# Half of batch 1's second product as seven block products, DVE's work of that stretch reordered, and the states' rows read two batches together

## The chip, the cores and the metric

The kernel runs on one core of a Trainium2 chip. The metric is the device time of one execution in microseconds, lower is better. TensorE (PE) multiplies into PSUM, VectorE (DVE) and ScalarE (ACT) compute and empty PSUM, GpSimd (POOL) copies and adds between SBUF tiles, and SyncE (SP) issues most of the DMAs. Each engine takes its instructions in the order in which the program issues them, and semaphores order the engines among each other.

## What is computed

For each of 8 batches and 8 heads, x (512 rows of 64) and state (32 rows of 64) read each other by attention; the 544 rows of each batch then go through a feed-forward layer, 512 to 2048 to 512, with a leaky ReLU.

```python
scores = scale * np.matmul(x, state.transpose(0, 1, 3, 2))
a = softmax(scores); xread = np.matmul(a, state)        # 512 rows a batch
scores2 = scale * np.matmul(state, x.transpose(0, 1, 3, 2))
a2 = softmax(scores2); sread = np.matmul(a2, x)         # 32 rows a batch
rows = np.concatenate([xread, sread], axis=2)           # heads side by side: 512 columns
h = rows @ w_in; out = np.maximum(0.01 * h, h) @ w_out
```

## The kernel before, in words

All five engines follow an order written out by hand (manual_schedule): the program's text is each engine's queue. bfloat16 goes into the products, PSUM holds float32.

Work on the 512 rows of a batch. a_scores writes both heads' score halves (the "sc" bank pair). For x's rows, a_shift takes the maximum per block of 32 (block_max), spreads it (a transpose) and subtracts it, a_exp is ACT's exp, and a_probs sums, inverts, spreads and multiplies into aT. For the states' rows, a_max2, a_exp2 (ACT, with the sum accumulated) and a_probs2 give a2, which a_a2t transposes by DMA on SP. xread is never formed: a_m multiplies the state by w_in into M (four chunks of 512 columns, each copied out of PSUM by ACT or DVE), and ff1 multiplies aT by M and applies the leaky ReLU on ACT, writing hT, 16 slots of 128 columns.

The second product, hT by w_out, has two forms. piece is the plain one: four matmuls of 512 columns for a block of 128 rows, four pieces to a block. Fast, with Batch on top, is Strassen's scheme in Winograd's form, seven block products for eight: weights_sum makes four sums of blocks of w_out (tw), Fast.sums makes four sums of blocks of hT (su) on DVE, unit is one step of one product (two matmuls of 256 columns for a batch's 512 rows), save copies a bank to SBUF on ACT, join adds a bank and a saved one on DVE, and one addition goes to POOL. Two banks ("py") carry the seven products, in the order 1, 2, 6, 5, 7, 3, 4: products 6 and 3 add into the bank in which products 1 and 5 already stand, after those were saved.

The main loop runs over b = 2 to 7, and over 16 slots s in each. Slot s holds ff1 of batch b for 128 columns, and a filling of second-product units: of batch b - 1, and from about slot 10 of batch b itself (PACE). The next batch's attention (nxt) lies on DVE and ACT in the same slots: a_scores and a_shift in slot 1, a_max2 in slot 3, a_exp in 5, a_exp2 and a_probs in 7 and 8, a_probs2 in 11; three chunks of its M come in slot 10. ff1, the rows' product and chunk 2 of M share the two "ph" banks in turn. Batches 0 and 1 come ahead of the loop. Batch 0's second product and batch 1's are done by pieces; of batch 1's, six pieces lie ahead of the loop and the last ten in slots 0 to 9 of b = 2 (the list std).

The states' 32 rows are read by a_sread_rows: 32 small matmuls per batch (a2T by xb), copied by ACT to sr_n and transposed by DMA (sread_t) into sr_t; batch 7's by a_sread. It is called for batch 0 in slot 1 of b = 2, for batches 1 and 2 in slot 10 of b = 2, and for batch b in slot 10 of b = 3 to 6. All states' rows go through the feed-forward layer together at the end (FastIn and fs).

## Time and profile before

| | |
|---|---|
| three runs | 204.59, 204.79, 205.09 us; median 204.79 |
| the profiled execution | 204.49 us, of which the span in the profile is 202.7 |
| busy in the span | PE 197.0 us, DVE 151.4, ACT 143.7, POOL 39.7 |
| granted TensorE clock | 1.0 |
| bytes moved by DMA | 27.99 MB |
| PE matmuls of 128x256 in the second products, one | 109 ns apart |
| PE matmuls of 128x512, one | 216 ns apart |

A row of the timeline gives start and duration in us, engine, line of the kernel, operation, output tile from input tiles, shape, and how many are merged into it; a bracket gives idle time ahead of it and the engine that ended it. A row of a group gives the total, the mean duration in ns and the idle time ahead. Durations of matmuls overlap one another, so starts are used for them.

### The profile page before, as it was taken

Reading aid. Unit: us, or ns where it says so; the run is one execution under the profiler, and the core shown is the slowest. Engines: PE = TensorE matmul, PEld = TensorE weight load, DVE = VectorE, ACT = ScalarE, POOL = GpSimd, SP = SyncE. Lnnn points to the kernel's source line nnn. Section 1 sums busy time; section 2 is a strip of 40 time slices with the busy share of each in tenths; the row PEclk is TensorE's granted clock in tenths of the full one; section 3 lists DMA queues with packets and bytes.
Section 4 is the critical chain, followed back from the end, with each engine's and each line's share of the span. In section 5 each row is a group of like instructions: output and inputs, shape, how many; then the busy total and the mean of one; then the engine's idle time right before and its main releaser. Section 6 shows DMA issues by size and latency. Waiting matters only on the chain.

```text
span 202.7 us, 4755 instructions
## 1 busy us (share of the span) xinstructions
PE 197.0 (97%) x1964; PEld 126.0 (62%) x1964; DVE 151.4 (75%) x230; ACT 143.7 (71%) x265; POOL 39.7 (20%) x66
## 2 busy tenths in 40 slices
PE   7899999999999999999999999999999999999993
PEld 2543544444344567766776767766767677799882
DVE  1677679599799969976996699769968853686612
ACT  3458848589869796978697878788778856467710
POOL 8831002021005005200251040200020002004250
PEclk9999999999999999999999999999999999999999
DMA  6999996999477895537946795250017100410035
GB/s 189 223 207 277 229 298 113 141 303 245 53 175 214 114 275 109 103 125 253 118 29 181 240 127 105 103 159 5 0 57 198 27 0 32 178 55 0 3 89 170
DMA packets 39733, 27.99 MB, mean 138 GB/s; under 512 B 25312, under 2 KB 36704, under 8 KB 39712
## 3 DMA queue, kind: packets, MB, share of 16 engines
q1 hardware_dynamic: 34512, 20.88, 44.6%
q0 software_dynamic: 4912, 6.55, 15.8%
q10 hardware_dynamic: 288, 0.26, 0.6%
q8 instruction: 15, 0.25, 0.5%
q14 instruction: 6, 0.05, 0.1%
HBM read 17.30 MB, written 8.91 MB: 129 GB/s over the span
## 4 chain that ended last, share of the span: by engine, by line
PE 96%; DVE 1%; ACT 1%; issue 0%
PE yq L557 36%; PE ph L372 23%; PE py L487 10%; PE pm L351 4%; PE pyw L487 3%; PE pf L441 3%; PE yu L557 3%; PE pspin L132 3%; PE ph L804 2%; PE sc L206 1%; PE psn L318 1%; PE phw L383 1%; PE php L804 1%; DVE M L365 1%; ACT xT L666 1%; PE scn L695 0%
## 5 line engine op out<-in xcount | busy, mean ns | idle before, releaser
L377 ACT ACTIVATE hT<-ph 128x512 bf16<-128x512 f32 x108 | 63.5, 604 | 22.0 <-PE ph L372 21.4
L372 PE MATMUL ph<-aT,M 128*128 128x512 bf16 x216 | 62.3, 379 | 0.0
L557 PEld LDWEIGHTS <-su 128*128 128x128 bf16 x416 | 39.7, 98 | 14.5 <-DVE su L546 1.7
L557 PEld LDWEIGHTS <-hT 128*128 128x128 bf16 x288 | 27.7, 98 | 11.7 <-issue 1.1
L557 PE MATMUL yq<-tw_xf,su 128*128 128x256 bf16 x192 | 27.2, 273 | 0.0
L105 POOL CAST xb<-xl 128x512 bf16<-128x512 f32 (+1 forms) x21 | 14.4, 724 | 65.2 <-PE ph L372 40.6
L557 PE MATMUL yq<-w_out_bf,hT 128*128 128x256 bf16 x192 | 27.0, 273 | 0.0
L372 PEld LDWEIGHTS <-M 128*128 128x128 bf16 x216 | 21.0, 98 | 9.3 <-issue 0.8
L546 DVE TENSOR_TENSOR su<-hT 128x1024 bf16<-128x1024 bf16 x24 | 16.8, 700 | 10.5 <-ACT hT L377 10.5
L487 PE MATMUL py<-w_out_bf,hT 128*128 128x512 bf16 x96 | 24.2, 379 | 0.0
L487 PEld LDWEIGHTS <-hT 128*128 128x128 bf16 x128 | 12.1, 98 | 14.6 <-issue 0.9
L627 POOL TENSOR_TENSOR yo<-sv,sv 128x512 f32<-128x512 f32 x6 | 7.8, 1300 | 54.1 <-ACT sv L566 42.7
L569 DVE TENSOR_TENSOR yo<-yq,sv 128x512 f32<-128x512 f32 x17 | 11.6, 685 | 6.5 <-PE yq L557 6.5
L566 ACT COPY sv<-yq 128x512 f32<-128x512 f32 x24 | 13.9, 585 | 2.0 <-PE yq L557 1.4
L365 ACT CAST M<-pm 128x1024 bf16<-128x1024 f32 x13 | 13.2, 1014 | 0.9 <-PE pm L351 0.8
L557 PE MATMUL yq<-w_out_bf,su 128*128 128x256 bf16 x96 | 13.1, 273 | 0.0
L557 PE MATMUL yq<-tw_x,su 128*128 128x256 bf16 x96 | 13.1, 272 | 0.0
L557 PE MATMUL yq<-tw_x,hT 128*128 128x256 bf16 x88 | 12.1, 273 | 0.0
L274 ACT ACTIVATE e<-sc,mcols 128x512 bf16<-128x512 f32 x16 | 11.1, 696 | 0.0
L216 DVE TRANSPOSE_TENSOR_REDUCE mrow<-sc 128x32 f32<-128x1024 f32 x7 | 8.7, 1245 | 2.4 <-PE sc L206 2.4
L266 DVE TENSOR_REDUCE mcol<-sc 128x2 f32<-128x1024 f32 x8 | 9.7, 1215 | 0.0
L247 DVE STREAM_TRANSPOSE qb<-qh 128x1024 bf16<-128x1024 bf16 x7 | 8.7, 1245 | 0.2
(147 smaller groups left out, 271.3 us busy)
## 6 DMA issues: line engine op xcount, KB each, us to landing
xl<-in_x_dram SPq DMA_DIRECT2D x5, 1024.0 KB, 7.1
out_dram<-yo SPq DMA_DIRECT2D x10, 512.0 KB, 3.0
w_in_bf<-in_moe_w_in_dram POOLq DMA_DIRECT2D x4, 512.0 KB, 9.1
w_out_bf<-in_moe_w_out_dram POOLq DMA_DIRECT2D x4, 512.0 KB, 17.0
out_dram<-ysb SPq DMA_DIRECT2D x8, 256.0 KB, 5.1
xf<-in_x_dram SPq DMA_DIRECT2D x2, 512.0 KB, 4.8
x<-in_x_dram POOLq DMA_DIRECT2D x2, 512.0 KB, 13.8
xl<-in_x_dram POOLq DMA_DIRECT2D x1, 1024.0 KB, 19.8
```

The costliest lines, as they stand in the source:

```text
L105: copy(xs[b][:, :, h0:h1].rearrange("p t h d -> p h t d"), xl[b][:, h0:h1].rearrange("p h (t d) -> p h t d", t=NT),)
L216: nc.vector.tensor_reduce(out=m1[:], in_=flat.rearrange("p (c j) -> p c j", j=NS), axis=AX.X, op=ALU.max, apply_transpose=True,)
L266: nc.vector.tensor_reduce(out=m2[:], in_=a.sc[:], axis=AX.X, op=ALU.max, negate=True)
L274: nc.scalar.activation(out=a.e2[:, g], in_=a.sc[:, g, :], func=AF.Exp, bias=a.m2s[:, g:g + 1], scale=SCALE, accum_out=a.r2[:, g:g + 1],)
L365: copy(a.M[:, :, cols], pm[:])
L372: nc.tensor.matmul(ph[:], lhsT=a.M[:, g, P * j:P * (j + 1)], rhs=a.aT[:, g, :], start=(g == 0), stop=(g == 1),)
L377: nc.scalar.activation(out=hT[:, j, :], in_=ph[:], func=AF.Prelu, alpha=0.01)
L487: nc.tensor.matmul(y.py, lhsT=hT[:, j, P * i:P * (i + 1)], rhs=w_out_bf[:, j, :], start=(j == 0), stop=(j == 15),)
L546: (eng or nc.vector).tensor_tensor(out=S[n][:, ms], in0=u[:, ms], in1=v[:, ms], op=op)
L557: nc.tensor.matmul(bank[:, i, :], lhsT=lhs[:, m, P * i:P * (i + 1)], rhs=rhs[:, m, :], start=(first and m == 0 and (i == 0 or of is not No ...
L566: copy(t[:], bank)
L569: nc.vector.tensor_tensor(out=dst, in0=bank, in1=self.sv[n][:], op=ALU.add)
```

## The change

Rows 256 to 511 of batch 1's h1 (a block of two row blocks) take a new class Half: the seven block products with one 128-row matmul per unit (56 matmuls of 256 columns) in place of eight pieces, seven units a slot in slots 2 to 9 of b = 2. Its sums, saves and joins come with it. The sums of w_out move ahead: two to the end of batch 0, one to the end of batch 1, one to slot 4 of b = 2. In b = 2 the next batch's attention is spread anew: the row maxima's spreading in slot 1, the subtraction and a_max2 in slot 4, a_exp in 6, a_exp2 in 8 and 9, a_probs' reciprocal in 9 and its multiplication after slot 10's copies. For batches 0 to 6, a2 stays unnormalised (a2 is e2 itself), its reciprocals are kept in qall, and DVE multiplies them in when it copies the rows' product out of PSUM, where ACT copied before. The rows of batches 1 and 2, 3 and 4, 5 and 6 are read together, in slot 1 of b = 3, 5 and 7. e2 and a2T have three buffers, sread_t takes three batches and then four, and the order of the two "py" banks is turned in even batches instead of odd ones.

```diff
@@ -140,6 +140,7 @@
     st_t = [consts.tile([P, hi - lo, P], BF16, name=f"st_t{lo}") for lo, hi in groups]
     sr_t = consts.tile([P, B, NK, NS], BF16, name="sr_t")
     sr_n = {}
+    qall = consts.tile([P, B, 2], FP32, name="qall")
     stb0 = consts.tile([P, 4, D], BF16, name="stb0")
@@ -219,9 +220,12 @@
         )
         return m1
-    def block_sub(flat, m1, n):
+    def block_rows(m1, n):
         m1b = att.tile([P, n, NS], FP32, name="mrowb", tag="mrowb", bufs=1)
         nc.vector.transpose(m1b[:], m1[:, :, None].to_broadcast([P, n, NS]))
+        return m1b
+
+    def block_sub(flat, m1b, n):
         sh = att.tile([P, n * NS], FP32, name="sh", tag="sh", bufs=1)
         nc.vector.tensor_tensor(
             out=sh[:], in0=flat, in1=m1b[:].rearrange("p c j -> p (c j)"), op=ALU.subtract,
@@ -233,7 +237,7 @@
         nc.scalar.activation(out=e1[:], in_=sh[:], func=AF.Exp, scale=SCALE)
         return e1
-    def block_probs(dst, e1, n):
+    def block_recip(e1, n):
         r1 = att.tile([P, n], FP32, name="r1", tag="r1")
         nc.vector.tensor_reduce(
             out=r1[:], in_=e1[:].rearrange("p (c j) -> p c j", j=NS),
@@ -243,6 +247,9 @@
         q1h = att.tile([P, n], BF16, name="qh", tag="qh")
         with nc.allow_low_precision(reason="one rounding, of the finished reciprocal"):
             nc.vector.reciprocal(q1h[:], r1[:])
+        return q1h
+
+    def block_probs(dst, e1, q1h, n):
         q1b = att.tile([P, n, NS], BF16, name="qb", tag="qb", bufs=1)
         nc.vector.transpose(q1b[:], q1h[:, :, None].to_broadcast([P, n, NS]))
         nc.vector.tensor_tensor(
@@ -250,16 +257,22 @@
             in1=q1b[:].rearrange("p (g c) j -> p g (c j)", g=2), op=ALU.mult,
         )
-    def a_shift(a):
+    def a_shift(a, part=None):
         flat = a.sc[:].rearrange("p g c -> p (g c)")
-        a.sh = block_sub(flat, block_max(flat, NB), NB)
+        if part != 1:
+            a.mb = block_rows(block_max(flat, NB), NB)
+        if part != 0:
+            a.sh = block_sub(flat, a.mb, NB)
     def a_exp(a):
         a.e1 = block_exp(a.sh, NB)
-    def a_probs(a):
-        a.aT = att.tile([P, 2, S], BF16, name="aT", tag="aT")
-        block_probs(a.aT[:], a.e1, NB)
+    def a_probs(a, part=None):
+        if part != 1:
+            a.q1h = block_recip(a.e1, NB)
+        if part != 0:
+            a.aT = att.tile([P, 2, S], BF16, name="aT", tag="aT")
+            block_probs(a.aT[:], a.e1, a.q1h, NB)
     def a_max2(a):
         m2 = att.tile([P, 2], FP32, name="mcol", tag="mcol")
@@ -269,7 +282,7 @@
     def a_exp2(a, g):
         if g == 0:
-            a.e2 = att.tile([P, 2, S], BF16, name="e2", tag="e2")
+            a.e2 = att.tile([P, 2, S], BF16, name="e2", tag="e2", bufs=3)
             a.r2 = att.tile([P, 2], FP32, name="r2", tag="r2")
         nc.scalar.activation(
             out=a.e2[:, g], in_=a.sc[:, g, :], func=AF.Exp,
@@ -278,17 +291,19 @@
     def a_probs2(a):
         nc.vector.tensor_scalar(out=a.r2[:], in0=a.r2[:], scalar1=1e-9, scalar2=None, op0=ALU.add)
-        q2 = att.tile([P, 2], FP32, name="qc", tag="qc")
-        nc.vector.reciprocal(q2[:], a.r2[:])
-        a.a2 = att.tile([P, 2, S], BF16, name="a2", tag="a2")
-        for g in range(2):
-            nc.vector.tensor_scalar(
-                out=a.a2[:, g, :], in0=a.e2[:, g, :],
-                scalar1=q2[:, g:g + 1], scalar2=None, op0=ALU.mult,
-            )
+        q2 = qall[:, a.b]
+        nc.vector.reciprocal(q2, a.r2[:])
+        a.a2 = a.e2
+        if a.b == B - 1:
+            a.a2 = att.tile([P, 2, S], BF16, name="a2", tag="e2", bufs=3)
+            for g in range(2):
+                nc.vector.tensor_scalar(
+                    out=a.a2[:, g, :], in0=a.e2[:, g, :],
+                    scalar1=q2[:, g:g + 1], scalar2=None, op0=ALU.mult,
+                )
     def a_a2t(a):
-        a.a2T = att.tile([P, 2, NT, P], BF16, name="a2T", tag="a2T")
+        a.a2T = att.tile([P, 2, NT, P], BF16, name="a2T", tag="a2T", bufs=3)
         nc.sync.dma_start_transpose(
             a.a2T[:].rearrange("p g i q -> p (g i) q"), a.a2[:].rearrange("p g s -> p (g s)")
         )
@@ -320,16 +335,18 @@
                             lhsT=a.a2T[:, g, i, NS * k:NS * (k + 1)], rhs=a.xb[:, i, 2 * k + g, :],
                             start=(i == 0), stop=(i == NT - 1),
                         )
-        c, b0 = divmod(some[0].b, 4)
+        c, b0 = (0, some[0].b) if some[0].b < 3 else (1, some[0].b - 3)
         if c not in sr_n:
             sr_n[c] = consts.tile([P, 4, P], BF16, name=f"sr_n{c}", tag=("st0f", "stf2")[c])
-        nc.scalar.copy(
-            sr_n[c][:, b0:b0 + len(some)], ps[:].rearrange("p u g d -> p u (g d)")
+        u0, n = some[0].b, len(some)
+        nc.vector.tensor_tensor(
+            out=sr_n[c][:, b0:b0 + n].rearrange("p u (g d) -> p u g d", g=2), in0=ps[:],
+            in1=qall[:, u0:u0 + n, :, None].to_broadcast([P, n, 2, D]), op=ALU.mult,
         )
     def sread_t(c, n):
         nc.sync.dma_start_transpose(
-            sr_t[:, 4 * c:4 * c + n].rearrange("p b k n -> p b (k n)"),
+            sr_t[:, 3 * c:3 * c + n].rearrange("p b k n -> p b (k n)"),
             sr_n[c][:, :n].rearrange("p b q -> p (b q)"),
         )
@@ -527,7 +544,7 @@
         def __init__(self, hT, q, homes, saved):
             self.q, self.sub = q, q // P
-            hv = hT[:].rearrange("p (m k) s -> p m k s", k=2)
+            hv = hT.rearrange("p (m k) s -> p m k s", k=2)
             self.A = {(r, k): hv[:, :, k - 1, q * (r - 1):q * r] for r in (1, 2) for k in (1, 2)}
             self.homes, self.saved, self.S = homes, saved, {}
             self.sv = {}
@@ -575,7 +592,7 @@
     class Batch:
         def __init__(self, b, hT):
             saved = {n: (spool, t, 1) for n, t in ((1, "sv1"), (6, "sv6"), (5, "sv1"), (7, "sv7"))}
-            self.b, self.f = b, Fast(hT, 2 * P, [(spool, f"su{n}", 1) for n in range(4)], saved)
+            self.b, self.f = b, Fast(hT[:], 2 * P, [(spool, f"su{n}", 1) for n in range(4)], saved)
             self.units = [(n, m) for n in (1, 2, 6, 5, 7, 3, 4) for m in range(NM)]
             own = [(n, m) for n in (1, 2) for m in range(6)] + [(1, 6), (2, 6), (1, 7)]
             assert len(own) == OWN
@@ -596,8 +613,8 @@
         def open(self, n):
             if n in (1, 2):
                 if not self.bank:
-                    ts = [psum.tile([P, 2, HC], FP32, name="yq", tag="py") for _ in range(2)]
-                    if self.b % 2:
+                    ts = [psum.tile([P, self.f.sub, HC], FP32, name="yq", tag="py") for _ in range(2)]
+                    if self.b % 2 == 0:
                         ts.reverse()
                     for k, t in zip((1, 2), ts):
                         self.bank[k] = t[:]
@@ -635,6 +652,22 @@
             elif n == 4:
                 f.join(self.yo(1)[:, :, :HC], bank, 7)
                 self.out(1)
+
+    class Half(Batch):
+
+
+        def __init__(self, hT):
+            super().__init__(1, hT)
+            self.f.__init__(hT[:, :, 2 * P:], P, self.f.homes, self.f.saved)
+            self.units = [(n, m) for n in (1, 2, 6, 5, 7, 3, 4) for m in range(NM)]
+
+        def yo(self, r):
+            if r not in self.yos:
+                self.yos[r] = ypool.tile([P, 1, DM], FP32, name="ysb", tag="ysb", bufs=3)
+            return self.yos[r]
+
+        def out(self, r, cols=slice(0, DM), i=None, eng=nc.sync):
+            eng.dma_start(rows_of(1)[2 + r], self.yo(r)[:, 0, :])
     OWN = 15
     PACE = (1, 4, 4, 4, 3, 4, 4, 3, 4, 4, 4, 4, 3, 4, 3, 3)
@@ -888,6 +921,9 @@
         cast_x(3, h, h + 2, POO)
     a_probs2(a0)
     a_a2t(a0)
+    weights_open()
+    weights_sum(2)
+    weights_sum(1)
@@ -919,6 +955,7 @@
     a_probs2(a2)
+    weights_sum(0)
     pm = [a_m(a2, 1, "big"), a_m(a2, 2, "sc")]
     m_evict(a2, 1, pm[0], VEC)
     m_evict(a2, 2, pm[1], SCA)
@@ -927,8 +964,7 @@
-    before = None
-    weights_open()
+    before, half = None, Half(h1)
     for b in range(2, B):
         hT = hpool.tile([P, 16, S], BF16, name="hT", tag="hT")
         a = att_of[b]
@@ -936,7 +972,9 @@
         now = Batch(b, hT)
         std = []
         if b == 2:
-            std = [(i, 3) for i in range(2)] + [(i, jq) for i in range(2, NT) for jq in range(4)]
+            std = [(i, 3) for i in range(2)]
+            for n in (0, 1):
+                half.f.sums(n)
         def fill(s):
             n = (PACE2 if b == 2 else PACE)[s]
@@ -953,7 +991,6 @@
             if s == 0:
                 if b + 2 < B:
                     load_x(b + 2, nc.sync)
-                    open_xb(b + 2)
                 a_a2t(a)
                 if before:
                     for n in (0, 1):
@@ -964,9 +1001,15 @@
                 m_evict(a, 3, a_m(a, 3, "big"), SCA)
                 if b == 2:
                     a_sread_rows([a0])
-                if nxt is not None:
+                elif b % 2:
+                    a_sread_rows([att_of[b - 2], att_of[b - 1]])
+                if b == 2:
+                    half.f.sums(2)
+                    a_shift(nxt, 0)
+                elif nxt is not None:
                     a_shift(nxt)
                 if b + 2 < B:
+                    open_xb(b + 2)
                     for h in range(0, H, 2):
                         cast_x(b + 2, h, h + 2, POO)
                 if before:
@@ -974,24 +1017,18 @@
             elif s == 3:
                 if before:
                     before.f.sums(3)
-                if nxt is not None:
+                if nxt is not None and b > 2:
                     a_max2(nxt)
-                if b == 2:
-                    weights_sum(0)
-                    weights_sum(2)
             elif s == 4:
                 if b == 2:
                     state_t(1)
                 elif b == 4:
-                    sread_t(0, 4)
+                    sread_t(0, 3)
                 elif b == 7:
-                    sread_t(1, 3)
+                    sread_t(1, 4)
             elif s == 8:
                 if nxt is None:
                     a_sread(a)
-                if b == 2:
-                    weights_sum(1)
-                    weights_sum(3)
             elif s == 12:
                 for n in range(3):
                     now.f.sums(n, 0, 4)
@@ -1007,7 +1044,12 @@
                 a_open(att_of[b + 2], b + 2)
                 a_xt_dma(att_of[b + 2])
             if nxt is not None:
-                if s == 5:
+                if b == 2 and s < 11:
+                    if s == 6:
+                        a_exp(nxt)
+                    elif s in (8, 9):
+                        a_exp2(nxt, s - 8)
+                elif s == 5:
                     a_exp(nxt)
                 elif s in (7, 8):
                     a_exp2(nxt, s - 7)
@@ -1020,16 +1062,26 @@
             if std:
                 i, jq = std.pop(0)
                 piece(1, h1, i, jq)
+            elif b == 2 and half.units:
+                half.run(7)
+                if s == 4:
+                    a_shift(nxt, 1)
+                    half.f.sums(3)
+                    weights_sum(3)
+                    a_max2(nxt)
+                elif s == 9:
+                    a_probs(nxt, 0)
             elif s != 11:
                 fill(s)
             if s == 10 and nxt is not None:
-                a_sread_rows([a1, a2] if b == 2 else [a])
                 pm0 = a_m(nxt, 0, "big")
                 pm1 = a_m(nxt, 1, "sc")
                 pm2 = a_m(nxt, 2, "ph")
                 for g, copy in enumerate((VEC, SCA)):
                     copy(nxt.M[:, g, 2 * DM:3 * DM], pm2[g][:])
                 m_evict(nxt, 0, pm0, SCA)
+                if b == 2:
+                    a_probs(nxt, 1)
         before = now
@@ -1038,8 +1090,8 @@
     hs = hpool.tile([P, 16, B * NS], BF16, name="hs", tag="hT")
     for n in (0, 1):
         before.f.sums(n, 4, 8)
-    fs = Fast(hs, P, [(att, "sh", 1), (att, "mrowb", 1), (att, "xT", 2), (att, "xT", 2)],
-              {1: (att, "e1", 1), 6: (att, "qb", 1), 5: (att, "e2", 2), 7: (att, "e2", 2)})
+    fs = Fast(hs[:], P, [(att, "sh", 1), (att, "mrowb", 1), (att, "xT", 2), (att, "xT", 2)],
+              {1: (att, "e1", 1), 6: (att, "qb", 1), 5: (att, "e2", 3), 7: (att, "e2", 3)})
     fi.hT = hs
     for n in (1, 2, 6, 5, 7, 3, 4):
         for r in range(2):
```

## Prediction

> **What bounds the kernel now.** I read the page's busy shares first, then the chain of waits in order of time, then the timeline of TensorE, DVE and ACT around the stretch that is changed.
>
> ```profile
> PE 197.0 (97%) x1964; PEld 126.0 (62%) x1964; DVE 151.4 (75%) x230; ACT 143.7 (71%) x265; POOL 39.7 (20%) x66
> PEclk9999999999999999999999999999999999999999
> PE 96%; DVE 1%; ACT 1%; issue 0%
> ```
>
> TensorE is busy for 97% of the span at the full granted clock, and the chain that ended last is 96% TensorE. From the start times of its matmuls I took each step minus that form's usual step: after 20 us it hardly waits for another engine, apart from the three short waits of term (c). So the end moves by the TensorE time removed, less any new wait on TensorE.
>
> ```profile
> 33.34 3.45 PE pyw L487 x16
> 67.01 0.63 PE psn L318 x64
> 189.64 6.11 PE yu L557 x56
> ```
>
> In these lines of the chain, 16 matmuls of 512 columns take 3.45 us (216 ns each), 64 of the rows' product 0.63, and 56 of 256 columns 6.11 (109 each). The last is exactly the form that the change puts in: seven products of eight matmuls, on the states' rows.
>
> ```profile
> 65.76 0.59 PE L372 MATMUL ph<-aT,M 128*128 128x512 bf16 x2
> 66.19 0.82 PE L557 MATMUL yq<-w_out_bf,hT 128*128 128x256 bf16 x6
> 66.94 0.70 PE L318 MATMUL psn<-xb,a2T 128*32 128x64 bf16 x64
> 67.57 0.99 PE L351 MATMUL pm<-w_in_bf,st_t 64*32 64x512 bf16 x24
> 68.49 0.83 PE L557 MATMUL yq<-w_out_bf,hT 128*128 128x256 bf16 x6
> 69.28 1.02 PE L372 MATMUL ph<-aT,M 128*128 128x512 bf16 x4
> 70.14 0.60 PE L557 MATMUL yq<-w_out_bf,hT 128*128 128x256 bf16 x4
> 70.70 0.59 PE L372 MATMUL ph<-aT,M 128*128 128x512 bf16 x2
> ```
>
> This is TensorE's timeline at slots 10 to 13 of stage 2 (the pass of the loop with b = 2); starts are what counts.
>
> **The removed and added TensorE work.**
>
> (a) Eight pieces of four matmuls (32 x 0.2156 = 6.90) become 56 of 256 columns (6.11): -0.79. A slot of slots 2 to 9 shrinks from 1.295 (55.40 to 65.76 over eight) to 0.432 + 7 x 0.109 = 1.195. From this, slot 2 still starts at 55.40, slot 6 at 60.18, slot 7 at 61.38, and slot 10 would at 64.96.
>
> The Trainium skill, TensorE: Matmul & The Clock Gate, Part 3 (The mechanism), says that a weight load overlaps running matmuls only where the row groups differ, which would speak against more and narrower matmuls. The trace disagrees: 56 full-height loads of 98 ns lie beside the 6.11 us.
>
> (b) Rows' products. Before: 64 in slot 10 of stage 2 (66.94 to 67.57, 0.63) and 32 in slot 10 of stages 3 to 6 (87.54 to 87.89, 0.35 each): 2.03. After: 64 in slot 1 of stages 3, 5 and 7. The 32 of batch 0, in slot 1 of stage 2 before and after, cost 0.34 (54.18 to 54.52); 32 more cost 0.63 - 0.35 = 0.28; so 0.62 each, 1.86. Net -0.17.
>
> (c) Three waits of stage 2 go with what made them. The pm group takes 0.92 (67.57 to 68.49) against 0.80 in stage 3 (87.89 to 88.69), for ACT's late psn copy. At 69.28 six matmuls of 0.109 should have been over at 69.15: DVE's copy of pm2[0], queued behind two weight sums, started only at 68.61. At 70.70 TensorE is 0.12 late behind an ACT queue that the psn copy had set back. Together -0.37.
>
> **What new waits cost.** The other engines take their work in the order issued, so I walked each queue with start-to-start times of the old trace.
>
> ```profile
> 59.92 0.60 ACT L377 ACTIVATE hT<-ph 128x512 bf16<-128x512 f32 x1 [0.70 <-PE ph L372]
> 60.41 1.05 ACT L233 ACTIVATE e<-sh 128x1024 bf16<-128x1024 f32 x1
> 61.36 0.58 ACT L497 COPY ysb<-py 128x512 f32<-128x512 f32 x1
> ```
>
> (d) In slot 6 ACT's queue is ff1's relu, a_exp (moved from slot 5), then save(5). The relu starts 0.64 after its first matmul (56.69 to 57.33 in the old trace): 60.82. The exp starts 0.49 later (59.92 to 60.41), 61.31; save(5) another 0.95 later (60.41 to 61.36), 62.26, and takes the 0.372 of the 128x256 copies of sv at L566: 62.63, with 0.06 for the release 62.69. The third product adds into the bank that save(5) reads, and TensorE is there at 61.38 + 0.432 + 5 x 0.109 = 62.36. **+0.33.** Nothing else of TensorE is between; before, eight pieces used no save.
>
> ```profile
> 45.96 1.23 DVE L238 TRANSPOSE_TENSOR_REDUCE r<-e 128x32 f32<-128x1024 bf16 x1
> 47.22 0.18 DVE L242 TENSOR_SCALAR r<-r 128x32 f32<-128x32 f32 x1
> 47.44 0.35 DVE L245 RECIPROCAL qh<-r 128x32 bf16<-128x32 f32 x1
> 68.61 0.69 DVE L1031 CAST M<-pm 128x512 bf16<-128x512 f32 x1 [0.26 <-PE pm L351]
> ```
>
> (e) In slot 9 a_probs' first part stands behind the join of the fourth product, which needs the last of the 56 matmuls, and DVE's copy of pm2[0] stands behind both; ff1 of slot 11 needs that bank. From the end of slot 9: 0.20 to the join (a copy starts 0.31 after the last matmul's start), 0.345 for it (0.424 at L569 on 128x256, the next starts 0.08 earlier), 1.27 + 0.22 + 0.27 for reduce, scalar and reciprocal, 0.67 of the copy (ff1 started at 69.28): 2.975. TensorE needs, without psn and (c), 69.28 - 65.76 - 0.63 - 0.25 = 2.62. **+0.35.**
>
> (f) Stage 1: DVE idles 1.61 us before its reduce at 40.66. Two weight sums there (L523, 1.14 and 1.25 apart) replace two multiplies (0.62) and run 0.1 over; ACT follows and ff1's banks have no slack at 49.85. Bounds 0 and 0.16; I take **+0.05**, as ACT had 0.04 in hand.
>
> **Edits costed at nothing.** The first weight sum (1.23) ends at 51.5, under the 0.99 us that DVE waited for pm at 51.71; uncovered it would hold only M columns that slot 4 needs. The multiplies of a2 (0.62 per batch) go from an engine that idles 1.5 to 1.8 us per stage. sums(0) and (1) of the half end at 54.65, sums(2) at 55.6, sums(3) at 61.2 under the casts of POOL; products need them from 58.4, 61.05 and 62.36. join(2) starts at 58.6, ends 0.7 before its bank is wanted. The split a_shift leaves sh at 60.2, an exp that starts at 61.31. a_max2 ends at 64.1, where ACT's first exp2 is due. a_probs' second part ends at 70.2, needed at 72.5. The rows' copy on DVE (128x256 with a broadcast; bounded by 0.372 of ACT's and 0.69 of 128x512, taken as 0.42) waits in stages 3, 5 and 7 behind two sums and a join and ends at 76.5 by stage 3's old clock; its bank is wanted in slot 3, 78.06. Uncovered it would cost its excess three times. Behind it, the shift is 0.14 later against TensorE, with 0.32 spare at exp2. On SP's queue, a2T's transposes no longer wait for DVE (53.89 becomes about 51.5), so load_x(4) and POOL's casts come 2.4 us earlier; the last sread_t waits for DVE's copy of slot 1 and has six slots. Cast_x now stands on POOL behind the rows' product, and its data land later than that anyway.
>
> **Sum.** -0.79 - 0.17 - 0.37 + 0.33 + 0.35 + 0.05 = -0.60, so the profiled execution's 204.49 (span 202.7 and 1.8 around it) becomes 203.9. That execution lay 0.30 under the median of the three, 204.79; against the median the forecast is 204.2. 0.3% (0.61 us) is about what a measurement of this kernel can tell from no change, and the forecast lies on that line.
>
> **Rivals.**
>
> *The waits (d) and (e) are covered.* If ACT and DVE run a little ahead of my walk, only gains stay: -1.33, 203.5. For it: each is a third of a microsecond, and idle time lies just ahead on both engines. Against: both queues are fixed orders of rows that vary little. Chance 0.20.
>
> *DVE's chain is longer.* The scalar row was 0.43 once (62.79) instead of 0.18, the rows' copy may take 0.69, and stage 7's rows have 0.09 spare on ACT: 0.3 to 0.7 more, 204.5 to 204.9. Chance 0.13.
>
> *Slower: POOL's casts shut DVE out.* They now fall on sums(3) and the last weight sum, about 60.2 to 63.1. If DVE stood until they end, sums(3) would end at 63.8 and the third product start 1.16 later still; a_max2 would end after 66.2, both exp2 after 68.4, and the "sc" bank be 0.55 late for pm1 (in place of (e)): 204.2 + 1.36 = 205.6. It decides once sums(3) ends after 62.7. Against: under casts in the old trace the same sums took 1.03 for 0.69 and 1.62 for 1.36, a stretch and no stop. Chance 0.07. The Trainium skill, SBUF — State Buffer, on the two sides of SBUF, calls that port pair an exclusive lock held for one whole instruction; by it DVE could lose one cast's time at each turn, and the rows agree with the milder reading.
>
> *Slower: weight loads bind.* If 24 more loads of 98 ns were not hidden, +2.35: 206.5. The 6.11 us speak against it. Chance 0.02; this is the page's rule under (a).
>
> **How the numbers follow.** The forecast as walked holds 0.58, from 203.9 to 204.5, split 0.27 beyond the line and 0.31 within it. Faster: 0.27 + 0.20 = 0.47. Within 0.3%: 0.31 + 0.11 of the longer chain = 0.42. Slower: 0.02 + 0.07 + 0.02 = 0.11. The range runs from the covered case, 203.4, to the end of the longer chain, 204.9, and leaves out the two slower rivals and the edges.
>
> **What would show it.** Slots 2 to 9 of stage 2 with steps of 1.195 and 56 matmuls at 0.109; one wait of about 0.33 on ACT at the third product, one of about 0.35 on DVE ahead of slot 11's ff1; stage 4 shorter by 0.35, stages 3 and 5 longer by 0.27 than their 21.05. Wrong would be: steps above 1.2 without a wait, sums(3) or a_max2 as releasers, or a psn bank that holds ff1 in slot 3.

## The result, and the profile after

The changed kernel takes 203.90 us (median of nine runs, 203.71 to 204.28); the kernel before, beside it, 204.71 (nine runs, 204.25 to 205.32). The ratio is 0.9964, with a 95% interval from 0.9953 to 0.9975: faster than before beyond doubt, by 0.36% (0.40% by the medians). That is just beyond the 0.3% line, but the interval reaches back across it. The profiled execution is 203.81 us with a span of 202.0, against 204.49 and 202.7. The forecast was 203.9 for the profiled execution and 204.2 against the median.

First the busy shares and the clock of the page, then the shares of the chain by engine:

```profile
PE 195.3 (97%) x1988; PEld 127.4 (63%) x1988; DVE 151.3 (75%) x227; ACT 142.2 (70%) x261; POOL 39.1 (19%) x67
PEclk9999999999999999999999999999999999999999
...
PE 89%; DMA 5%; POOL 2%; DVE 1%; ACT 1%; issue 0%; POOLq 0%; ACTq 0%
```

TensorE still bounds the kernel at the full clock, with 1.7 us less busy time; 24 matmuls more are the 56 for 32 of term (a). The chain's 5% of DMA is the load of w_in in the first 16 us, through which this execution's chain happens to be followed back; ACT and DVE have 1% each.

The times below need a mark. The first "sc" matmul of a batch's a_scores is in every kernel, and the one of batch 2, in the stage ahead of the loop (stage 1), started anywhere from 39.68 to 40.54 us over the thirteen profiled executions, with no visible order by the edits (40.18 before, 40.14 after). So I count from that mark, step by step, to the first "sc" matmul of batch 3 (slot 1 of stage 2), 4, 5, 6 and 7, and to the start of the last matmul:

| us | stage 1 | stage 2 | stage 3 | stage 4 | stage 5 | stage 6 on | total |
|---|---|---|---|---|---|---|---|
| before | 13.44 | 21.07 | 21.05 | 21.05 | 21.05 | 61.13 | 158.80 |
| after | 13.65 | 19.82 | 21.31 | 20.67 | 21.31 | 61.37 | 158.13 |

The gain is all in stage 2 (-1.25); stage 1 gives back 0.21, and the stages from 3 on give back 0.38. By windows cut at these marks, after's stages 2, 3 and 4 (length first, then busy time of each engine):

```profile
53.79:73.61 19.82, 19.67 (x198) 12.68 (x197) 17.66 (x27) 16.63 (x33) 4.03 (x6) 1.00 0.86 204
73.61:94.92 21.31, 21.31 (x251) 14.89 (x250) 17.06 (x25) 16.56 (x31) 3.55 (x5) 1.00 0.44 118
94.92:115.59 20.67, 20.67 (x186) 14.32 (x185) 16.89 (x24) 16.55 (x31) 3.55 (x5) 1.00 0.58 154
```

TensorE is busy in all of stages 3 and 4: their lengths are work. Stage 2 has 0.15 us in which it stands idle. The chain in order of time shows where (start, duration, what):

```profile
60.94 0.45 PE yq L574 x4
...
61.47 1.05 ACT e L237
62.52 0.27 ACT sv L583
62.79 0.04 issue
62.84 0.38 PE yq L574 x2
...
66.69 0.77 PE pm L368 x24
67.46 0.76 PE yq L574 x6
68.22 1.00 PE ph L389 x4
```

That is wait (d): a_exp (e, L237), then save(5) (sv, L583), then the third product. From the start times, TensorE lost 0.314 us there (the page's busy time models a longer end of the matmul ahead, so it counts half of that as idle). The pm group takes 0.77 where it took 0.92. Slots 2 to 9 start 1.195 apart (ff1 at 59.15, 60.35, 61.54 in TensorE's timeline).

### The profile page after: what moved, and what is told of

It reads as the page before. It is cut to its first block, busy times and chain, and to the rows that moved or that the text cites. A ratio compares the mean times of both kernels' runs of the same rounds, so it can differ in the third digit from the quotient of the medians.

```text
span 202.0 us, 4793 instructions
## 1 busy us (share of the span) xinstructions
PE 195.3 (97%) x1988; PEld 127.4 (63%) x1988; DVE 151.3 (75%) x227; ACT 142.2 (70%) x261; POOL 39.1 (19%) x67
## 4 chain that ended last, share of the span: by engine, by line
PE 89%; DMA 5%; POOL 2%; DVE 1%; ACT 1%; issue 0%; POOLq 0%; ACTq 0%
PE yq L574 39%; PE ph L389 23%; PE py L504 7%; DMA w_in_bf<-in_moe_w_in_dram 5%; PE pm L368 4%; PE pyw L504 3%; PE pf L458 3%; PE yu L574 3%; PE ph L837 2%; PE sc L207 1%; PE psn L333 1%; PE phw L400 1%; POOL w_in_bf L118 1%; DVE M L382 1%; ACT e L237 1%; PE pxt L887 0%
## 5 line engine op out<-in xcount | busy, mean ns | idle before, releaser
L574 PEld LDWEIGHTS <-su 128*128 128x128 bf16 x448 | 42.8, 98 | 15.1 <-DVE su L563 0.8
L574 PE MATMUL yq<-tw_xf,su 128*128 128x256 bf16 x208 | 29.5, 273 | 0.0
L574 PE MATMUL yq<-w_out_bf,hT 128*128 128x256 bf16 x208 | 29.3, 273 | 0.0
L563 DVE TENSOR_TENSOR su<-hT 128x1024 bf16<-128x1024 bf16 x26 | 18.2, 700 | 11.1 <-ACT hT L394 11.0
L105 POOL CAST xb<-xl 128x512 bf16<-128x512 f32 (+1 forms) x21 | 12.5, 633 | 56.2 <-DMA xl<-in_x_dram 30.8
L583 ACT COPY sv<-yq 128x512 f32<-128x512 f32 (+1 forms) x28 | 15.4, 554 | 2.1 <-PE yq L574 1.4
L504 PE MATMUL py<-w_out_bf,hT 128*128 128x512 bf16 x64 | 16.0, 379 | 0.0
L574 PE MATMUL yq<-w_out_bf,su 128*128 128x256 bf16 x104 | 14.3, 273 | 0.2 <-ACT sv L583 0.2
L574 PE MATMUL yq<-tw_x,su 128*128 128x256 bf16 x104 | 14.3, 273 | 0.0
L563 DVE TENSOR_TENSOR su<-su,hT 128x1024 bf16<-128x1024 bf16 x13 | 9.0, 691 | 0.4
```

Source lines behind the costliest of these rows:

```text
L105: copy(xs[b][:, :, h0:h1].rearrange("p t h d -> p h t d"), xl[b][:, h0:h1].rearrange("p h (t d) -> p h t d", t=NT),)
L504: nc.tensor.matmul(y.py, lhsT=hT[:, j, P * i:P * (i + 1)], rhs=w_out_bf[:, j, :], start=(j == 0), stop=(j == 15),)
L563: (eng or nc.vector).tensor_tensor(out=S[n][:, ms], in0=u[:, ms], in1=v[:, ms], op=op)
L574: nc.tensor.matmul(bank[:, i, :], lhsT=lhs[:, m, P * i:P * (i + 1)], rhs=rhs[:, m, :], start=(first and m == 0 and (i == 0 or of is not No ...
L583: copy(t[:], bank)
```

## The experiments

Each kernel is the changed kernel with one edit. Ratios are to the kernel before, run beside it; stages and totals are counted as above, and "against after" is the difference from 158.13. Medians measured at different times differ by up to 0.36 us for kernels whose steps are the same (203.90 after, 203.54 in experiment 3), so the small differences are read from the steps.

**1. a_exp behind save(5)** (tests (d))

```diff
-                    if s == 6:
-                        a_exp(nxt)
-                    elif s in (8, 9):
+                    if s in (8, 9):
...
                 half.run(7)
+                if s == 6:
+                    a_exp(nxt)
```

> The changed kernel with one edit: in stage 2, slot 6, a_exp is issued behind the slot's seven units, so ACT does save(5) first. Theory (the third product waits for save(5), which stands behind the exp): the wait of 0.31 us before the third product goes; save(5) ends near 61.9 and TensorE passes there at 62.5. Up to 0.15 may come back at pm2[1], whose bank waits for a relu that the second a_exp2 holds up. So 0.16 to 0.31 us less than the changed kernel's 203.9. Rival (ACT is late there for another reason, or the wait only moves): no change.

Measured: 203.38 us, ratio 0.9950 (0.9937 to 0.9962). Stage 2 is 19.51 in place of 19.82, the others unchanged: -0.30 in all. ACT's timeline:

```profile
60.95 0.60 ACT L394 ACTIVATE hT<-ph 128x512 bf16<-128x512 f32 x1 [0.34 <-PE ph L389]
61.45 0.37 ACT L583 COPY sv<-yq 128x256 f32<-128x256 f32 x1
61.70 1.07 ACT L237 ACTIVATE e<-sh 128x1024 bf16<-128x1024 f32 x1
```

The save comes a microsecond earlier, the chain of the stretch is TensorE alone, and the exp, 0.23 later, makes nobody late. So (d) is this order on ACT, and its whole price.

**2. The second weight sum later** (tests (f))

```diff
     weights_sum(2)
-    weights_sum(1)
...
             a_max2(a2)
+            weights_sum(1)
```

> The changed kernel with one edit: weights_sum(1) is issued behind a_max2 of batch 2 in stage 1, not at the end of batch 0. Theory (the second weight sum makes the reduce of batch 2 late, ACT's exp with it, and two relus miss ff1's banks in slots 14 and 15): the waits of 0.19 and 0.06 us before ff1 in slots 14 and 15 of stage 1 go, 0.2 to 0.25 us less than 203.9; nothing comes back, as aT of batch 2 ends near 50.9 and is needed at 51.8, and DVE idles 0.69 us before the first join. Rival (the stage is late by ACT's or SP's own order): no change.

Measured: 203.41 us, ratio 0.9949 (0.9935 to 0.9963); stage 1 is 13.45 as before the change, all else as in after: -0.20. The rows of after (DVE, ACT and TensorE in turn) and then those of this kernel show the path:

```profile
38.37 1.22 DVE L540 TENSOR_TENSOR tw_x<-w_out_bf 128x2048 bf16<-128x2048 bf16 x1
39.70 1.23 DVE L540 TENSOR_TENSOR tw_xf<-w_out_bf,tw_x 128x2048 bf16<-128x2048 bf16 x1
40.84 1.24 DVE L217 TRANSPOSE_TENSOR_REDUCE mrow<-sc 128x32 f32<-128x1024 f32 x1
...
44.71 1.06 ACT L237 ACTIVATE e<-sh 128x1024 bf16<-128x1024 f32 x1 [0.19 <-DVE sh L230]
48.85 1.11 ACT L394 ACTIVATE hT<-ph 128x512 bf16<-128x512 f32 x2
...
49.53 1.08 PE L389 MATMUL ph<-aT,M 128*128 128x512 bf16 x4
```

```profile
40.68 1.25 DVE L217 TRANSPOSE_TENSOR_REDUCE mrow<-sc 128x32 f32<-128x1024 f32 x1 [1.03 <-PE sc L207]
...
44.56 1.06 ACT L237 ACTIVATE e<-sh 128x1024 bf16<-128x1024 f32 x1
48.71 1.11 ACT L394 ACTIVATE hT<-ph 128x512 bf16<-128x512 f32 x2
...
49.40 1.06 PE L389 MATMUL ph<-aT,M 128*128 128x512 bf16 x4
```

In after, the second sum ends behind the scores, so the reduce follows it with no idle time; ACT's exp waits 0.19 for DVE, and that runs on through ACT's queue to the relus at 48.85 and ff1 at 49.53. With one sum DVE has 1.03 us to spare.

**3. DVE and ACT change copies** (tests (e))

```diff
-                for g, copy in enumerate((VEC, SCA)):
+                for g, copy in enumerate((SCA, VEC) if b == 2 else (VEC, SCA)):
```

> The changed kernel with the two copies of M's chunk 2 in stage 2 exchanged: ACT copies pm2[0] and DVE pm2[1]. Theory A (ff1 of slot 11 takes the bank of pm2[1], whose copy is ACT's in the changed kernel and ends at 68.14, 0.06 before ff1): ff1 of slot 11 now waits for DVE's copy, which ends near 68.43, and is 0.25 to 0.3 us later. Theory B, the prediction's (ff1 of slot 11 takes the bank of pm2[0]): it waits for ACT's copy as now, no change.

Measured: 203.54 us, ratio 0.9957 (0.9945 to 0.9970); total -0.02 against after. The wait before slot 11's ff1 is 0.101 in place of 0.136. The matmuls and copies of the stretch, in this kernel's timeline of all engines:

```profile
67.20 0.83 PE L574 MATMUL yq<-w_out_bf,hT 128*128 128x256 bf16 x6
67.33 0.59 ACT L1081 CAST M<-pm 128x512 bf16<-128x512 f32 x1 [0.69 <-PE pm L368]
67.60 0.63 DVE L1081 CAST M<-pm 128x512 bf16<-128x512 f32 x1
...
67.97 1.02 PE L389 MATMUL ph<-aT,M 128*128 128x512 bf16 x4
```

ff1 starts 0.05 after ACT's copy ends (67.92) and well ahead of the end of DVE's (68.23). So it is ACT's copy that it waits for, here too. The traces say the same in another way: here, before and after the change, and in experiment 4, the first matmul of slot 11's ff1 waits on the semaphore that ACT counts up, and that of slot 12's ff1 on DVE's. Which half ACT copies does not matter to this wait; the run does not tell why the bank that comes first follows ACT.

**4. a_probs' first part behind the copies** (tests (e) once more)

```diff
-                elif s == 9:
-                    a_probs(nxt, 0)
...
                 if b == 2:
-                    a_probs(nxt, 1)
+                    a_probs(nxt)
```

> The changed kernel with a_probs of batch 3 whole behind slot 10's copies in stage 2, so that DVE's copy of chunk 2 stands right behind the last join and starts with pm, near 67.5 in place of 67.8. Theory (the wait of 0.14 us before ff1 of slot 11 is the round trip of ACT's copy, and DVE's chain has some 0.2 us in hand): the wait stays at 0.13 to 0.15. The prediction's term (e) (DVE's chain from the last join sets it): the wait goes. By either, DVE is 1.8 us later into stage 3: aT is done near 72.1, just ahead of 72.4, and behind it the rows' copy, the third sum and a_max2 have little left, so stage 3 may take 0 to 0.8 us more.

Measured: 203.58 us, ratio 0.9950 (0.9931 to 0.9969), a total of 158.13 like after's, and the same wait of 0.136. DVE now idles ahead of its copy, which starts with ACT's (67.85 and 67.88, both behind the pm group), and slot 11's ff1 comes no earlier. Nor did anything become late by the 1.8 us of a_probs that moved behind it. So DVE's chain in slots 9 to 11 sets nothing, in either direction.

**5. Slot 11 longer** (tests whether the waits of 0.136 and 0.119 can be covered)

```diff
-    PACE2 = (0,) * 10 + (3, 3, 2, 2, 2, 3)
+    PACE2 = (0,) * 10 + (3, 4, 2, 2, 2, 2)
```

> The changed kernel with one unit of batch 2's second product moved from slot 15 of stage 2 to slot 11, ahead of ff1 (PACE2 ends 3, 4, 2, 2, 2, 2). Theory (the 0.14 us wait of ff1 in slot 11 is the round trip of a copy of chunk 2, which eight matmuls cover and six do not, as in stages 3 to 6): the wait goes, and most of the 0.12 before ff1 of slot 13 with it: 0.14 to 0.25 us less than 203.9. Rival (DVE's chain from the last join sets it, as term (e) had it): ff1 stays where it is and only the order of work changes: no change.

Measured: 203.62 us, ratio 0.9961 (0.9947 to 0.9974); total -0.07, less than expected. Eight matmuls ahead of ff1 in place of six do cover both waits (neither is left above 0.05), but 0.07 came back at 72.20, in the middle of a slot's second-product units, and the pm group lost 0.06 (0.83 for 0.77). In the combination below, the pace part is worth more: that kernel's total is 0.65 less, of which (d) and (f) explain 0.50, and its pm group keeps its 0.77.

**6. The rows where they were** (takes the regrouping back; the copy stays on DVE)

```diff
-                elif b % 2:
-                    a_sread_rows([att_of[b - 2], att_of[b - 1]])
...
             if s == 10 and nxt is not None:
+                a_sread_rows([a1, a2] if b == 2 else [a])
```

> The changed kernel with the rows' products back in slot 10 (batches 1 and 2 in stage 2, one batch in each of stages 3 to 6), copied by DVE with the multiplication. Theory (TensorE's time for the groups is 2.03 us in the old places and 1.86 in the new, and in stage 2 a rows' copy stands on DVE behind a_probs' first part while chunk 2 of M waits for its bank): 0.17 us more, and 0.3 to 0.55 for that wait: 0.45 to 0.7 us more than 203.9. Rival (the regrouping is worth its matmuls alone): 0.17 us more.

Measured: 204.83 us, ratio 1.0009 (0.9995 to 1.0024): the whole gain is gone. The steps are 13.66, 20.97, 21.14, 21.08, 21.08 and 61.16, 0.95 more than after. Stage 2 pays 1.15: 0.63 are the 64 matmuls, as in before, and 0.51 are a wait in the middle of the pm group, which the chain of this kernel lays on DVE:

```profile
65.95 0.42 DVE ysb L586
66.38 1.16 DVE r L242
67.54 0.02 issue
67.56 0.19 DVE r L246
67.75 0.02 issue
67.78 0.35 DVE qh L249
68.13 0.29 DVE sr_n L342
68.42 0.04 issue
68.46 0.41 PE pm L368 x7
```

The rows' product and the pm group share the bank; DVE's copy out of it stands behind a_probs' first part. Moving the rows to slot 1, where DVE is free enough, is what lets DVE take that copy and lets a_probs be split as it is. The 0.95 is more than the 0.45 to 0.7 expected, though the wait itself was within its bounds: the regrouping is worth 0.25 and not 0.17, and from stage 3 on this kernel gets back only 0.20 of the 0.38, because DVE's copy lengthens the pm groups there too (0.89 and 0.83 in stages 3 and 4, where before had 0.80 and 0.81).

**7. Pieces in place of the seven products** (undoes (a), and (d) with it)

```diff
-    before, half = None, Half(h1)
+    before, half = None, None
...
-            std = [(i, 3) for i in range(2)]
-            for n in (0, 1):
-                half.f.sums(n)
+            std = [(i, 3) for i in range(2)] + [(i, jq) for i in range(2, NT) for jq in range(4)]
...
-            elif b == 2 and half.units:
-                half.run(7)
...
-                    half.f.sums(3)
```

> The changed kernel with batch 1's rows 256 to 511 by eight pieces again; its sums, saves and joins go, all else stays (the weight sums in their new places, the attention of batch 3 in its new slots, the rows in pairs). Theory (term (a) is 0.79 us of TensorE and the only price that it brought into stage 2 is the 0.31 us wait for save(5)): slots 2 to 9 back at 1.295 us each, no wait at the third product, 0.48 us more than 203.9. Rivals: the seven products carry the whole gain (0.8 us more), or nothing (no change).

Measured: 204.44 us, ratio 0.9987 (0.9976 to 0.9998); total +0.49 against after, all of it in stage 2 (20.31). That is 0.79 of matmuls less the 0.31 of (d), which has no save to wait for here: 0.48.

**8. The attention where it was** (with the seven products in place)

```diff
-                    a_shift(nxt, 0)
+                    a_shift(nxt)
...
-                if nxt is not None and b > 2:
+                if nxt is not None:
                     a_max2(nxt)
...
-                if b == 2 and s < 11:
-                    if s == 6:
-                        a_exp(nxt)
-                    elif s in (8, 9):
-                        a_exp2(nxt, s - 8)
-                elif s == 5:
+                if s == 5:
                     a_exp(nxt)
...
-                    a_shift(nxt, 1)
...
-                    a_max2(nxt)
-                elif s == 9:
-                    a_probs(nxt, 0)
```

> The changed kernel with the attention of batch 3 in stage 2 at the slots of the kernel before: a_shift whole in slot 1, a_max2 in 3, a_exp in 5, a_exp2 in 7 and 8, a_probs whole in 7; the half's third sum and the last weight sum stay in slot 4, behind the first join. Theory (the new order is there to keep the joins ahead of the attention on DVE): the first join stands behind the subtraction and a_max2, until about 61.2, and the fifth product waits 1.3 us for its bank; a_probs then holds the last two joins, up to 0.6 us more at slot 10; the wait for save(5) goes: 1.0 to 1.9 us more than 203.9, slower than the kernel before. Rival (DVE's order is immaterial since TensorE's work sets the end): no change to 0.3 us less.

Measured: 205.66 us, ratio 1.0050 (1.0031 to 1.0070): slower than the kernel before. Stage 2 is 21.82, 2.01 longer than after's. TensorE's timeline shows the two places, and DVE's what stood ahead:

```profile
61.82 0.60 PE L574 MATMUL yq<-tw_xf,su 128*128 128x256 bf16 x4 [1.40 <-DVE ysb L586]
...
68.22 0.81 PE L574 MATMUL yq<-w_out_bf,hT 128*128 128x256 bf16 x6 [0.59 <-DVE ysb L586]
```

```profile
58.55 1.23 DVE L230 TENSOR_TENSOR sh<-sc,mrowb 128x1024 f32<-128x1024 f32 x1
59.69 1.22 DVE L279 TENSOR_REDUCE mcol<-sc 128x2 f32<-128x1024 f32 x1
60.94 0.51 DVE L281 TENSOR_SCALAR mcols<-mcol 128x2 f32<-128x2 f32 x1
61.35 0.41 DVE L586 TENSOR_TENSOR ysb<-yq,sv 128x256 f32<-128x256 f32 x1
...
65.86 1.25 DVE L254 STREAM_TRANSPOSE qb<-qh 128x1024 bf16<-128x1024 bf16 x1
67.14 0.69 DVE L255 TENSOR_TENSOR aT<-e,qb 128x1024 bf16<-128x1024 bf16 x1
67.75 0.75 DVE L586 TENSOR_TENSOR ysb<-yq,sv 128x256 f32<-128x256 f32 x2
```

Each join (ysb) empties a bank that the next product needs, and here it stands behind the subtraction and a_max2, and later behind the five instructions of a_probs. From the start times TensorE lost 1.56 and 0.76; less the 0.31 of (d), which is gone here, that is the 2.01, a little beyond the 1.0 to 1.9 expected. So the seven products without the new order lose more than they gain.

**9. The multiplication of a2 kept** (the copy of the rows' product stays on DVE, with nothing to multiply), and the same with edit 2

```diff
             a.a2 = att.tile([P, 2, S], BF16, name="a2", tag="e2", bufs=3)
+        if True:
             for g in range(2):
...
-        nc.vector.tensor_tensor(
...
+        VEC(sr_n[c][:, b0:b0 + n], ps[:].rearrange("p u g d -> p u (g d)"))
```

> The changed kernel with the multiplication of a2 kept on DVE for every batch (in place in e2, two of 128x512 per batch, 0.53 us more of DVE each) and the rows' copy without it. Theory (the multiplications that went were covered by DVE's idle time, so their going gained nothing): 0 to 0.1 us more than 203.9. Rival (DVE is near enough to the bound that 0.53 us a stage shows): up to 0.5 for each of stages 1 to 6, 0.5 to 2 us more.

> The multiplications of a2 kept on DVE, and weights_sum(1) behind a_max2 of batch 2 in stage 1. In the profile with the multiplications kept, stage 1 (from batch 2's scores to batch 3's) took 14.20 us against 13.65 of the changed kernel and 13.44 before. Theory (in stage 1 the multiplications matter only because two weight sums follow them ahead of batch 2's reduce): with one of the sums gone from there the reduce comes when its scores are ready, and stage 1 takes 13.4 to 13.5, stage 2 19.8 as in the changed kernel; 0.2 us less than 203.9. Rival (the multiplications cost by themselves, there or elsewhere): stage 1 at 13.9 or more, or stage 2 longer than 19.9.

Measured: 203.91 us, ratio 0.9961 (0.9947 to 0.9975), and 203.88, ratio 0.9967 (0.9955 to 0.9979). In the profile of the first, stage 1 takes 14.20, 0.55 more than in after, and every other step is that of after to 0.01: the multiplications, pushed ahead of the two sums, make ACT's exp wait 0.74 for DVE. With the second sum out of the way stage 1 is 13.44, and stage 2 takes 19.91, 0.09 more than after's: in slot 1 the group of M's chunk 3 starts at 53.43, 0.05 behind the end of DVE's copy of chunk 1, which stands later on DVE here. So the multiplications cost nothing from stage 3 on, and in stage 2 at most 0.09. The timed runs do not confirm the 0.55: the profiled execution of the first kernel, at 204.44, is the slowest of its five, and the two medians are alike and like after's 203.90. How much of it the other executions have stays open.

**10. Edits 1, 2 and 5 together**

> The changed kernel with the exp behind save(5), the second weight sum behind a_max2 of batch 2, and the longer slot 11. If the three waits are separate, their gains add: 0.5 to 0.75 us less than 203.9, 203.1 to 203.4. If they share a cause, or DVE or ACT is next late at chunk 2's banks, 0.2 to 0.5 less.

Measured: 203.53 us, ratio 0.9943 (0.9924 to 0.9962). The steps are 13.44, 19.37, 21.31, 20.67, 21.31 and 61.37: 157.48, which is 0.65 less than after and 1.32 less than before. It beats the kernel before clearly. By the steps the gains add, as expected; the median does not reach the 203.1 to 203.4 expected, nor the medians of experiments 1 and 2, measured at another time. Against the changed kernel the intervals of the two ratios overlap, and it is the steps that put it ahead.

## Why the prediction held, and where it was wrong

The direction and the profiled execution (203.9 forecast, 203.81 measured) were right. The ratio came out on the side of the 0.3% line that had the chance of 0.47, but its interval spans the line. By the prediction's terms, in us:

| term | forecast | measured | by |
|---|---|---|---|
| (a) seven products | -0.79 | -0.79 | steps of 1.195; experiment 7 |
| (b) rows regrouped | -0.17 | -0.25 | 0.63 out of stage 2; +0.38 from stage 3 on, forecast +0.46 |
| (c) three waits gone | -0.37 | -0.15 | pm group 0.92 to 0.77; the other two stayed |
| (d) ACT, third product | +0.33 | +0.31 | start times; experiment 1 |
| (e) DVE, slot 11's ff1 | +0.35 | 0 | experiments 3 and 4 |
| (f) stage 1 | +0.05 | +0.21 | experiment 2 |
| sum | -0.60 | -0.67 | steps from the mark |

**(a) and (d)** were walked row by row, and the sizes held to 0.02. save(5) was due at 62.63 and ended at 62.78; the 0.15 is the later start of the stretch (ff1 of slot 6 at 60.35 for 60.18). The Trainium skill, TensorE: Matmul & The Clock Gate, Part 3 (The mechanism), by which a weight load would not overlap matmuls of the same row groups, finds no support here: the slots kept 109 ns a matmul. The same section lets a load into the background weight buffer run ahead; which buffer the loads here took, no run shows.

**(c) and (e)** failed at the same step: who empties the bank that slot 11's ff1 takes first. The prediction laid before's wait of 0.13 on DVE's copy at 68.61, as queued behind two weight sums. The bracket of that very row speaks against it: DVE had stood idle for 0.26 us and was released by the pm group. ACT's copy in the kernel before:

```profile
68.65 0.58 ACT L1031 CAST M<-pm 128x512 bf16<-128x512 f32 x1 [0.54 <-PE pm L351]
```

It ended at 69.23, and ff1 followed at 69.28, while DVE's copy ran to 69.30. That wait is the pm group, then a copy of 0.58 on ACT, against six matmuls of 0.109 each; it needs no late engine, so it did not go (0.126 before, 0.136 after). Nor did the 0.119 before slot 13, though ACT no longer copies psn. After's rows, TensorE then DVE and ACT:

```profile
67.39 0.83 PE L574 MATMUL yq<-w_out_bf,hT 128*128 128x256 bf16 x6
68.20 1.02 PE L389 MATMUL ph<-aT,M 128*128 128x512 bf16 x4
...
67.80 0.63 DVE L1081 CAST M<-pm 128x512 bf16<-128x512 f32 x1
...
67.56 0.58 ACT L1081 CAST M<-pm 128x512 bf16<-128x512 f32 x1 [0.72 <-PE pm L368]
```

The DVE copy starts when the walk said, and ends at 68.43; ff1 has long begun at 68.20, 0.06 after ACT's copy. The second bank is asked for only at 68.63, 0.2 later than DVE's copy ends. The same misreading put 0.35 too much on in (e) and took 0.22 too much off in (c), so most of it cancelled. The sum was better than its parts, and that was luck. (The sum in (e) also slips by 0.02: 69.28 - 65.76 - 0.63 - 0.25 is 2.64, and the term would have been +0.34.)

**(f)** was under-sized by 0.16, and the bound above it (0.16) too low. Two things failed: the two sums ran 0.22 over and not 0.1 (from the mark, the reduce starts at 0.70 in after, 40.84 - 40.14, and at 0.48 in before, 40.66 - 40.18), and ACT had nothing in hand: its exp is 0.21 late by the same count, its relus 0.20, and ff1 with them.

**(b)** was right in its matmuls: stage 4 came out 0.38 shorter (forecast 0.35; the rest is the pm group, 0.77 for 0.81 without the rows' product ahead of it), stages 3 and 5 0.26 longer (forecast 0.27). What it did not see is what the regrouping protects: without it DVE's new place for the copy costs 0.51 in slot 10 (experiment 6).

**Costed at nothing.** The multiplications were free from stage 3 on, as said, and within 0.09 in stage 2; in stage 1, in the profiled execution, their removal makes the room for the weight sums (experiment 9). The reordering of DVE is no detail at nothing: it covers 2.01 us (experiment 8), which the prediction treated as given because the change brought it along.

**The rivals.** Covered waits: not so, (d) was there in full. A longer chain on DVE: no row showed it, and moving 1.8 us of it behind the copies changed nothing. POOL's casts did fall on sums(3) and the last weight sum, earlier than walked:

```profile
58.56 2.29 POOL L105 CAST xb<-xl 128x512 bf16<-128x512 f32 x4 [13.29 <-PE ph L389]
60.79 1.07 POOL L177 CAST stb<-stf 128x512 bf16<-128x512 f32 x1
...
60.34 1.05 DVE L563 TENSOR_TENSOR su<-hT,su 128x1024 bf16<-128x1024 bf16 x1
61.31 1.62 DVE L540 TENSOR_TENSOR tw_x<-tw_xf,w_out_bf 128x2048 bf16<-128x2048 bf16 x1
```

They took 1.05 and 1.62 (0.69 and 1.22 elsewhere), and sums(3) ended at 61.39, ahead of the 62.7 from which the rival decides. But the prediction's "a stretch and no stop" misreads how: the rows show turns. The casts of L105 end at 60.85, sums(3) 0.54 later; the next cast ends 0.47 after sums(3), the weight sum 1.07 after that cast. Where the same pairs meet in the kernel before, the gaps are the same (a cast ends at 79.82, an addition of DVE at 80.36, the next cast at 80.83). So each stops until the other engine's instruction under way has ended, and then runs; DVE loses at most the rest of one cast per turn, here 0.36 and 0.40, and does not wait for all of them.

**The number against the median.** I added 0.30 because before's profiled execution lay that far under its median. After's lies only 0.09 under, and before's median over nine runs is 204.71 and not 204.79. That offset, more than any term, is why 204.2 was forecast and 203.9 came. Of the 0.81 between the medians the steps explain 0.67.

## What to carry to other kernels

Before a wait is laid on the engine whose row looks late, read what that row itself waited for, and compare the end of every copy that could release the wait with the start of what waited: here the one that ended 0.05 us ahead was the cause, and the late row beside it had slack. Where an engine's queue has no idle time between a delay and the bottleneck, the delay arrives whole. A cheaper algorithm on the bottleneck engine is worth only what its joins and saves let through: here 0.79 us of matmuls stood against 2.01 us of order on DVE and 0.31 on ACT.

## What the runs showed of the hardware that was not expected

- Executions differ at the start: in eight profiles of kernels that are the same up to the mark in stage 1, it lay anywhere from 39.93 to 40.48, while steps that no edit touches repeat to 0.01 or 0.02. Profiles are better compared from a mark than from the start of the span.
- DVE's additions of two SBUF tiles and POOL's casts take turns, one instruction each, and both pay: in after 1.05 for 0.69 and 1.62 for 1.22 on DVE, and 1.07 for 0.61 for the fifth cast on POOL; in experiment 8 the second addition took 1.63, and the four casts beside the two additions 3.73 (2.29 in after). The subtraction, which reads one of its inputs from PSUM, took its usual 1.21 beside after's casts.
